# Seven block products for eight in the output matmul of a tuned kernel

What was changed: the second matmul of an expert block, `g @ w_out`, was made transposed for two batches at a time by Strassen's scheme. The block sums run on the vector engine, and the outputs are turned by 32x32 transposes on their way to memory.

## Chip, cores, metric

One core of one Trainium2 chip. The time is device microseconds (us) of a whole execution; a profiled execution also gives the span of the core, about 2 us less. Kernels that are compared ran on the same chip as runs of the kernel before. The engines are TensorE (PE), ScalarE (ACT), VectorE (DVE), GpSimd (POOL) and SyncE (SP, which only issues transfers here).

## The reference, cut

```python
# x: (8, 8, 512, 64) = batch, head, token, depth; state: (8, 8, 32, 64); all float32
scores = scale * x @ state^T;   a  = softmax(scores);   xread = a @ state
scores2 = scale * state @ x^T;  a2 = softmax(scores2);  sread = a2 @ x
y = concat([xread, sread], axis=tokens)    # (8, 544, 512) with the heads side by side
h = y @ w_in           # 512 x 2048
g = h * cos(h)
out = g @ w_out        # 2048 x 512, out is (4352, 512)
```

The weights arrive as float64 and are converted on the chip while batch 0 runs.

## The kernel before, the parts that matter

A batch (512 tokens) is worked in 16 steps, one per 128 columns of `w_in`. The attention of the next batch is cut into parts that stand in "slots" between the steps. In the traces each engine works through its instructions in the order in which the program names them: in batch 5 of the changed kernel the hidden tile named after the products starts behind them, at 607.45 us, although its buffer was read for the last time at 597.93.

```python
def hidden(t):                      # TensorE: h tile, 2 matmuls; only two h buffers
    for i in range(t.kn):
        nc.tensor.matmul(out=t.hp, lhsT=t.lhs(i), rhs=t.rhs(i), ...)
def gate(t):   nc.scalar.activation(t.q, t.hp, func=ACTF.Copy, bias=MAGIC)
def gate2(t):  nc.vector.scalar_tensor_tensor(out=t.q, ...)      # q = round(h) - h
def gate3(t):  nc.scalar.activation(..Abs); nc.scalar.activation(..Sin)
def gate4(t):  nc.vector.tensor_tensor(t.g, t.hp, t.q, op=ALU.mult)

def output(t):                      # TensorE: 4 matmuls per step, a few steps later
    for i in range(nt):
        nc.tensor.matmul(out=acc[i], lhsT=t.g[:, P * i:P * i + P],
                         rhs=w_out[:, t.f, :],
                         start=(t.f == 0), stop=(t.f == NF - 1))
    # ... after the last step: ACT evacuates acc[i], one DMA stores 128 rows of 2 KB

# parts of the attention of the next batch, in this order:
#   tokens 0..3, scores1, max2, spread1, shift, exps, sums, spread1, norm1   (EARLY)
#   turn 0,1, reads 0,1, keep, keep2                                         (LATE)
#   products 0..3                                                            (PRODS)
def products(self, nt, ...):        # 16 small matmuls into the one PSUM tile `at`
    self.per_head(stT, lambda rows, k: w_in[rows, k, cols], ...)
    nc.scalar.copy(sw_of[self.b, nt][...], at[...])
def exp2(self):                     # reads the same tile `at`
    nc.scalar.activation(self.z2[:, j], at[:, j], func=ACTF.Exp, ...)
def keep2(self):                    # transposes what keep (DVE) has just normalized
    nc.tensor.transpose(out=at[:, 1, 0:P], in_=self.sr..., identity=ident)
# ... the rest of the attention, the conversions and the loop are left out
```

In this kernel all four `products` of a batch come after its softmax; the pool of their results `sw` has six buffers.

## Time and profile before

| | before |
|---|---|
| time | 879.17 us median of 4 runs beside the changed kernel |
| span, PE busy, DVE busy, ACT busy | 877.2; 825.4; 330.8; 416.5 us |
| time of a steady batch (2 to 6) | 93.86 us, PE busy 93.86 us |

The page of the profile gives averages. More telling is a table of stretches: the span cut at the first gate instruction of each batch. The columns are start:end, length, then busy us (and count) of PE, weight loads, DVE, ACT and POOL, then the granted clock of TensorE as a fraction, the share of the DMA engines, and GB/s. Here are the starting stretch, batches 0 and 1, batch 4 and the rest after batch 7 (state tiles and end):

```profile
0.00:34.97 34.97, 12.53 (x60) 6.56 (x60) 17.29 (x26) 11.27 (x20) 3.13 (x10) 0.76 0.68 164
34.97:153.58 118.61, 96.72 (x362) 41.61 (x370) 86.22 (x113) 74.50 (x99) 0.00 (x0) 0.88 0.39 125
153.58:252.71 99.13, 97.40 (x379) 41.45 (x379) 32.06 (x47) 47.99 (x74) 0.00 (x0) 1.00 0.09 22
...
440.43:534.29 93.86, 93.86 (x331) 40.84 (x330) 31.94 (x47) 45.08 (x71) 0.00 (x0) 1.00 0.09 23
...
804.42:877.20 72.78, 67.06 (x216) 40.66 (x214) 13.52 (x32) 24.16 (x54) 0.00 (x0) 0.98 0.07 22
```

In batches 2 to 7 TensorE has no idle time at all. Apart from the start (22.4 us) and the end (5.7) it stands still only in batch 0, where the weights are converted, for 118.61 - 96.72 = 21.9 us, and for 1.7 us in batch 1.

### The profile page before, as it was taken

Reading aid. Unit: us, or ns where it says so; the run is one execution under the profiler, and the core shown is the slowest. Engines: PE = TensorE matmul, PEld = TensorE weight load, DVE = VectorE, ACT = ScalarE, POOL = GpSimd, SP = SyncE. Lnnn points to the kernel's source line nnn. Section 1 sums busy time; section 2 is a strip of 40 time slices with the busy share of each in tenths; the row PEclk is TensorE's granted clock in tenths of the full one; section 3 lists DMA queues with packets and bytes.
Section 4 is the critical chain, followed back from the end, with each engine's and each line's share of the span. In section 5 each row is a group of like instructions: output and inputs, shape, how many; then the busy total and the mean of one; then the engine's idle time right before and its main releaser. Section 6 shows DMA issues by size and latency. Waiting matters only on the chain.

```text
span 877.2 us, 7341 instructions
## 1 busy us (share of the span) xinstructions
PE 825.4 (94%) x2848; PEld 371.7 (42%) x2848; DVE 330.8 (38%) x485; ACT 416.5 (47%) x648; POOL 3.1 (0%) x10
## 2 busy tenths in 40 slices
PE   2549979999999999999999999999999999999997
PEld 1124334434444444444344434444444434445663
DVE  3666986244224422352224322442244222222121
ACT  2565674446345534463446444553446344433332
POOL 1000000000000000000000000000000000000000
PEclk8678989999999999999999999999999999999999
DMA  6743720030003000120003000300010001000100
GB/s 143 208 151 128 207 96 1 1 96 1 1 0 97 0 1 1 40 57 0 1 1 96 1 0 1 97 0 1 1 48 1 0 1 47 1 0 1 48 1 24
DMA packets 44418, 35.07 MB, mean 40 GB/s; under 512 B 35360, under 2 KB 35360, under 8 KB 44384
## 3 DMA queue, kind: packets, MB, share of 16 engines
q1 hardware_dynamic: 43168, 34.08, 13.6%
q10 hardware_dynamic: 1088, 0.26, 0.2%
q8 instruction: 22, 0.36, 0.2%
q0 software_dynamic: 128, 0.26, 0.1%
q14 instruction: 12, 0.10, 0.0%
HBM read 25.69 MB, written 8.91 MB: 39 GB/s over the span
## 4 chain that ended last, share of the span: by engine, by line
PE 88%; DVE 5%; ACT 5%; DMA 1%; issue 0%; SPq 0%; DVEq 0%; ACTq 0%
PE o L425 51%; PE h L395 28%; PE at L248 4%; PE at L325 2%; PE at L223 1%; PE at L310 1%; ACT q L410 1%; DMA x_b<-in_x_dram 1%; ACT q L409 1%; ACT e L166 1%; DVE q L404 1%; DVE w_in L183 0%; ACT q L401 0%; DVE m L261 0%; DVE w_out L183 0%; DVE spread L267 0%
## 5 line engine op out<-in xcount | busy, mean ns | idle before, releaser
L425 PE MATMUL o<-w_out,g 128*128 128x512 f32 x1088 | 494.3, 596 | 0.0
L425 PEld LDWEIGHTS o<-w_out,g 128*128 128x128 f32 x1088 | 203.4, 191 | 246.0 <-issue 242.7
L395 PE MATMUL h<-aT,sw 128*128 128x512 f32 x512 | 250.2, 612 | 0.2 <-ACT sw L357 0.2
L404 DVE SCALAR_TENSOR_TENSOR q<-q,h 128x512 f32<-128x512 f32 (+1 forms) x144 | 94.3, 655 | 333.0 <-ACT q L401 333.0
L401 ACT ACTIVATE q<-h 128x512 f32<-128x512 f32 (+1 forms) x144 | 82.5, 573 | 253.5 <-PE h L395 253.5
L415 DVE TENSOR_TENSOR g<-h,q 128x512 f32<-128x512 f32 (+1 forms) x144 | 95.2, 661 | 170.4 <-ACT q L410 170.3
L395 PEld LDWEIGHTS h<-aT,sw 128*128 128x128 f32 x512 | 95.7, 195 | 119.4 <-issue 110.4
L409 ACT ACTIVATE q<-q 128x512 f32<-128x512 f32 (+1 forms) x144 | 87.2, 606 | 107.6 <-DVE q L404 107.5
L410 ACT ACTIVATE q<-q,halfpi 128x512 f32<-128x512 f32 (+1 forms) x144 | 100.5, 698 | 4.5
L248 PE MATMUL at<-w_in,stT 64*32 64x512 f32 (+1 forms) x512 | 37.0, 620 | 8.4 <-ACT z L287 4.7
L357 ACT COPY sw<-at 128x1024 f32<-128x1024 f32 (+1 forms) x32 | 31.6, 987 | 24.9 <-PE at L248 24.9
L395 PE MATMUL h<-sT,w_in 128*128 128x256 f32 x128 | 30.2, 379 | 0.0
L431 ACT ACTIVATE ot<-o 128x512 f32<-128x512 f32 x34 | 19.3, 591 | 20.8 <-DMA out_dram<-ot 13.9
L395 PEld LDWEIGHTS h<-sT,w_in 128*128 128x128 f32 x128 | 24.3, 190 | 10.1 <-issue 5.3
L223 PE MATMUL at<-ident,x_b 128*128 128x128 f32 x112 | 17.9, 285 | 9.0 <-ACT xT L230 8.7
L223 PEld LDWEIGHTS at<-ident,x_b 128*128 128x128 f32 x112 | 14.3, 146 | 23.7 <-issue 11.6
L230 ACT COPY xT<-at 128x512 f32<-128x512 f32 x28 | 16.0, 572 | 10.5 <-PE at L223 10.5
L248 PEld LDWEIGHTS at<-w_in,stT 64*32 64x32 f32 x512 | 6.1, 107 | 34.8 <-issue 12.9
L267 DVE STREAM_TRANSPOSE spread<-m 128x1024 f32<-128x1024 f32 x16 | 19.8, 1235 | 0.0
L166 ACT ACTIVATE e<-raw 128x1024 f32<-128x1024 uint32 (+1 forms) x18 | 18.8, 1044 | 0.0
L325 PEld LDWEIGHTS at<-x_b,a2T 128*64 128x64 f32 x256 | 13.6, 136 | 12.1 <-issue 10.6
L325 PE MATMUL at<-x_b,a2T 128*64 128x128 f32 x256 | 17.5, 279 | 0.0
(53 smaller groups left out, 256.1 us busy)
## 6 DMA issues: line engine op xcount, KB each, us to landing
x_b<-in_x_dram SPq DMA_DIRECT2D x32, 256.0 KB, 4.7
raw<-in_moe_w_out_dram SPq DMA_DIRECT2D x8, 1024.0 KB, 4.9
out_dram<-ot SPq DMA_DIRECT2D x32, 256.0 KB, 2.1
raw<-in_moe_w_in_dram SPq DMA_DIRECT2D x6, 1024.0 KB, 5.3
raw<-in_moe_w_in_dram SPq DMA_DIRECT2D x4, 512.0 KB, 6.5
out_dram<-ot SPq DMA_DIRECT2D x8, 64.0 KB, 1.7
st<-in_state_dram ACTq DMA_DIRECT2D x4, 64.0 KB, 4.4
st<-in_state_dram POOLq DMA_DIRECT2D x4, 64.0 KB, 5.7
```

Source lines behind the costliest of these rows:

```text
L166: nc.scalar.activation(e, raw.bitcast(U32)[:, :, :, 0], func=ACTF.Copy, scale=2.0 ** -51, bias=2.0)
L223: nc.tensor.transpose(out=out[:, P * c:P * c + P], in_=self.x_b[:, c, 2 * k:2 * k + 2, :], identity=ident)
L248: nc.tensor.matmul(out=(to[j] if to else at[:, j])[Ns * k:Ns * k + Ns, 0:n], lhsT=w[D * j:D * j + D, self.b, Ns * k:Ns * k + Ns], rhs=r(sl ...
L325: nc.tensor.matmul(out=at[rows, 0, cols], lhsT=self.a2T[:, j, c, rows], rhs=x_c[:, j, k:k + 2], start=(c == 0), stop=(c == NC - 1), tile_p ...
L357: nc.scalar.copy(sw_of[self.b, nt][:, :, c0:c1], at[:, :, 0:c1 - c0])
L395: nc.tensor.matmul(out=t.hp, lhsT=t.lhs(i), rhs=t.rhs(i), start=(i == 0), stop=(i == t.kn - 1))
L401: nc.scalar.activation(t.q, t.hp, func=ACTF.Copy, bias=MAGIC)
L404: nc.vector.scalar_tensor_tensor(out=t.q, in0=t.q, scalar=MAGIC, in1=t.hp, op0=ALU.subtract, op1=ALU.subtract)
L409: nc.scalar.activation(t.q, t.q, func=ACTF.Abs)
L410: nc.scalar.activation(t.q, t.q, func=ACTF.Sin, bias=halfpi, scale=-TWO_PI)
L415: nc.vector.tensor_tensor(t.g[:, 0:t.n], t.hp, t.q, op=ALU.mult)
L425: nc.tensor.matmul(out=acc[i], lhsT=t.g[:, P * i:P * i + P], rhs=w_out[:, t.f, :], start=(t.f == 0), stop=(t.f == NF - 1))
```

## The change

The intent: TensorE is the bound, so do an eighth less of its output work. Two batches form a pair. The 2x2 blocks are batch by half of the hidden columns on one side and halves of `w_out` on the other. Seven products of blocks replace eight; the price is 128 subtractions of 128x512 on DVE, sums of weight blocks made once, more evacuations, and an output that comes out transposed.

A pair has four phases of eight steps: even batch first and second half (0, 1), odd batch first and second half (2, 3). Two products are put off: P7 (with the weight sum `s3`) and P4 (with the block `a22`) run beside phases 0 and 1 of the next pair, or beside the state tiles after the last one. Output follows its step by three steps.

```diff
-    swp = ctx.enter_context(tc.tile_pool(name="swp", bufs=6))
-    ops = ctx.enter_context(tc.tile_pool(name="ops", bufs=4, space=PSUM))
+    swp = ctx.enter_context(tc.tile_pool(name="swp", bufs=2))
+    ops = ctx.enter_context(tc.tile_pool(name="ops", bufs=1, space=PSUM))
+    acc = ops.tile([P, 2, 2, S], F32, name="o")      # banks MAIN and SIDE
 def output(t):
-    for i in range(nt):
-        nc.tensor.matmul(out=acc[i], lhsT=t.g[:, P * i:P * i + P],
-                         rhs=w_out[:, t.f, :], ...)
+    if t.phase == 0:
+        if product(MAIN, a11, t, i):
+            keep_product(pr.u, MAIN)
+        if pr.before:
+            p7(pr.before, i)
+    if t.phase == 1:
+        last = product(MAIN, a12, t, i)
+        if pr.before:
+            p4(pr.before, i)
+        # ... evacuate, store
+    if t.phase == 2:
+        if product(MAIN, s1, pr.b[0, i], i):
+            keep_product(pr.p5, MAIN)
+    if t.phase == 3:
+        last = product(MAIN, s2, pr.b[0, i], i)
+        product(SIDE, s4, t, i)
+        # ... evacuate, store
+def product(bank, w, g, i):         # 2 matmuls of 128x512 instead of 4 per step
+    for ch in range(2):
+        nc.tensor.matmul(out=acc[:, bank, ch], lhsT=w[:, i, P * ch:P * ch + P],
+                         rhs=g.g, start=(i == 0), stop=(i == NH - 1))
+def sums(t):                        # DVE: the block sums, in place in g
+    if t.phase == 2:
+        minus(pr.b[0, i].g, t.g, pr.b[0, i].g)
+    if t.phase == 3:
+        minus(pr.b[0, i].g, t.g, pr.b[0, i].g)
+        minus(pr.b[2, i].g, t.g, pr.b[2, i].g)     # and one more in sums2
+def store(b, half, ch, src):        # DVE 32x32 transposes, then rows of 32 floats
+    nc.vector.transpose(out=ot..., in_=src[:, ch]...)
+    nc.sync.dma_start(out=rows[:, :, c0:c0 + 32], in_=ot[32 * q:32 * q + 32]...)
+# slots of a batch b >= 1; two slots to a step:
+    at_ = {1: (b, "products", 1), 11: (b, "products", 2),
+           18: (b, "products", 3), 26: (b + 1, "products", 0)}
+    at_.update(zip((2, 3, 4, 5, 6, 7, 8, 9, 10, 12, 13, 14), E))
+    at_.update(zip((15, 16, 19, 20, 21, 22), L))
 # ... weight layout, conversions, state tiles and the tile generator are left out
```

With room for only two `sw` buffers, the products of a batch now stand among the softmax of the next one. `exps` is in slot 10 and `products 2` in slot 11.

## The prediction

> **What bounds the kernel now.** I read the page's busy times and slices first, then the costliest groups, then the timeline of TensorE, ScalarE (ACT) and VectorE (DVE) over some steady tiles and over the start.
>
> ```profile
> PE 825.4 (94%) x2848; PEld 371.7 (42%) x2848; DVE 330.8 (38%) x485; ACT 416.5 (47%) x648; POOL 3.1 (0%) x10
> PE   2549979999999999999999999999999999999997
> L425 PE MATMUL o<-w_out,g 128*128 128x512 f32 x1088 | 494.3, 596 | 0.0
> L395 PE MATMUL h<-aT,sw 128*128 128x512 f32 x512 | 250.2, 612 | 0.2 <-ACT sw L357 0.2
> ```
>
> TensorE is full from about 120 us to the end. Each matmul of the program leaves two records: the 544 output matmuls show as x1088. In the timeline the eight records of one tile's four output matmuls occupy 3.43 us, so **one output matmul costs 0.858 us**; the two hidden ones cost 1.72 us. A tile is 5.15 us of TensorE. A steady batch lasts 93.86 us (first gate instruction of batch 3 at 346.57, of batch 4 at 440.43): 16 x 5.15 = 82.4, plus 11.46 of attention (batch 7, which prepares nothing, lasts 82.4).
>
> Now the gate, which runs through ACT and DVE in turn:
>
> ```profile
> 401.92 0.60 ACT L401 ACTIVATE q<-h 128x512 f32<-128x512 f32 x1 [2.38 <-PE h L395]
> 402.55 0.69 DVE L404 SCALAR_TENSOR_TENSOR q<-q,h 128x512 f32<-128x512 f32 x1 [2.76 <-ACT q L401]
> 403.27 0.63 ACT L409 ACTIVATE q<-q 128x512 f32<-128x512 f32 x1 [0.75 <-DVE q L404]
> 403.93 0.72 ACT L410 ACTIVATE q<-q,halfpi 128x512 f32<-128x512 f32 x1
> 404.68 0.69 DVE L415 TENSOR_TENSOR g<-h,q 128x512 f32<-128x512 f32 x1 [1.45 <-ACT q L410]
> ```
>
> From the start of q to the end of g are 3.45 us. From one L404 to the next, when nothing else intervenes, are 0.72 + 0.66 + 0.75 + 0.61 = 2.75 us: **the gate loop**. Only two h buffers exist, and TensorE executes in order, so it can never be more than two tiles ahead of g. Today 2.75 against 5.15 leaves 2.4 us per tile, in which attention's ACT and DVE work hides. Where it does not hide, the start shows what happens:
>
> ```profile
> 48.23 1.11 PE L223 MATMUL at<-ident,x_b 128*128 128x128 f32 x4 [4.67 <-ACT xT L230]
> 118.30 1.96 PE L248 MATMUL at<-w_in,stT 64*32 64x512 f32 x16 [4.74 <-ACT z L287]
> ```
>
> The first says that two users of the tile `at` are serialized by the ACT copy of the first, though they use different banks. The second says that products placed behind the exponentials wait for these, because the exponentials read `at`.
>
> [...](691 for L415, 1218 for the 1024-wide L304 between SBUF tiles). So a block subtraction of 128x512 costs 0.69 us, spaced 0.61 (0.72 behind a result it needs). [...]exp follows sine's end after 1.3 us (284.16 to 285.48)[...]. I use the trace: load 1.28, exponentials 3.6 to 3.7 together, and another load ahead of the next sine. [...]after the 4.74 us above, the x16 group takes 1.96 us in place of 1.09. [...]the instruction order of the changed program keeps such waits.
>
> **The change, part by part.** I call one hidden tile a step, 16 to a batch.
>
> *Removed:* per pair of batches 128 output matmuls become 7 x 8 x 2 = 112, so 16 x 0.858 = 13.7 us, in four pairs **54.9 us**. If TensorE stayed full: 879 - 55 = 824.
>
> *Where it is removed:* two of the seven products of a pair move into the next pair's first batch (after batch 7: into the state tiles). So a TensorE step is 5.15 us in even batches, but in odd batches, steps 3 to 10, it has one product alone: 4 x 0.858 = 3.43 us. In the first pair it is 3.43 until step 11 of batch 1.
>
> *Added on DVE:* per pair 8 + 3 x 8 = 32 subtractions, 14 evacuations and totals, 8 transposes, 54 x about 0.65 = 35 us, or 140 us altogether, plus eight weight sums of 1.2 us and two more weight conversions. DVE goes from 331 to about 480 us, far from full. But in odd batches the subtractions lie in the gate loop: 2.75 + 0.71 = 3.46 us in steps 0 to 7 and about 4.75 in steps 8 to 15. So **in steps 3 to 10 loop and TensorE are even and all hiding room is gone**.
>
> *An odd batch that prepares a next one (3 and 5).* Time from the end of step 2's last product. DVE must do four evacuations, g, a subtraction and a store transpose, so gate2 of step 3 starts at 4.6. Then the loop carries max (1.2), row max (1.35), two to three transposes (0.65 each) and shift (1.2): sine of step 5 ends at 17.3. The exponentials end at 21.0. In the new order the products stand right behind them on TensorE, ahead of the next hidden tile; TensorE, finished at 12.0, idles **9 us**. Later in the same batch the transposes of step 8 wait for an ACT copy (2.0), the reads of step 9 for a copy behind a sine (2.0), the last transpose for the normalization on DVE (2.0). Sum 15, with a cold clock after the long gap about 17. The saving was 13.7.
>
> *An even batch (2, 4, 6):* at step 5 products wait for the exponentials, sine's end at 2.8 after TensorE's hidden tile plus 3.7, against 3.43 of products: 3.0 us. At step 10 four DVE evacuations precede g and the normalization, on which a transpose waits: 3.2 us. Sum 6.2. *Batch 7* prepares nothing: 1 us.
>
> *First pair.* A conversion step's loop is 2.75 + 2.6 (three DVE instructions ahead of gate2) = 5.35; pairs of `at` users cost 2.5 more. With 12 conversions, four plain steps, attention and a first step of 10.4, batch 0 takes 110 us against 118.6 (q at 34.97 to 153.58). Batch 1 has two conversions and seven weight sums in its loop besides: 52 to 54 us for steps 0 to 7, about 44 for the rest, 98 against 99.1. The first pair thus gains about 9 of its 41 us.
>
> *Sum.* Gate2 of batch 2 at 253.3 - 9 = 244. Batches 2 to 5: even 93.9 + 6.2 = 100, odd 80.1 + 15 = 95, twice 195, to 634. Batch 6: 100; batch 7: 68.6 + 3.7 + 1 = 73; to 807. From there the kernel before needs 72.2; add 32 matmuls of the two late products, 27.5, less 3.4 for a lag of three tiles in place of four: 903. Profile span to time is +2: **905**. Cold clocks would add some 5, slack that I missed takes away; I say 904.
>
> **Rivals.** *A: TensorE stays full.* For it: DVE at 38% and ACT at 47% have room on average, and the long phases have 5.15 us of TensorE a step. Against it: averages say nothing of an in-order loop with two h buffers. It gives 824 to 840. *B: only the loop in odd batches binds, copies and products mostly hide.* Losses would be about 6 us per odd batch and 20 in the first pair: about 860 to 880. For it: steady waits on `at` did not stop TensorE before. Against it: these had four output matmuls, 3.43 us, between them, now one pair, 1.72. *C: stores bind.* Outputs now leave in rows of 32 floats, 128 B, and DVE's transpose waits for one of two store buffers. If a group of four transfers takes over 6 us, several waits of a few us come into the loop at each of 16 groups: up to 925. Against it: input rows of 256 B came at about 200 GB/s, and transposes of one buffer are some 5 us apart. *D: the evacuations hold PSUM banks.* From the order a hidden tile and often another product lie between, so under 1 us each time.
>
> **Range and chances.** My sum of waits is 80 us against 55 saved, and its terms are chains, each good to perhaps a fifth; the first pair is uncertain by 8. Range 868 to 926. That a change built with so much care was tuned to pay speaks for A or B more than the profile does, hence faster 0.14, same 0.29, slower 0.57.
>
> **What would show it.** Right: TensorE busy near 770 us but at 84 to 87% of the span; output matmul records 960 in place of 1088; batches 3 and 5 each around 95 us and even ones around 100 between first gates; inside odd batches TensorE waiting for z about 9 us before `at` products, once a batch; in even ones about 3; the state tiles after batch 7 about 96 us. Wrong: no waits for z over 4 us outside batch 0 (A), odd batches near 85 (B), or DVE waiting for DMA in front of the transposes (C).

## The result

The changed kernel takes **954.26 us** (952.74 to 954.66, 4 runs) against 879.17: ratio 1.085 (95% interval 1.083 to 1.087), so 8.5% slower. Ratios here are the mean time of one kernel's fast runs over that of the other's of the same rounds, so not quite the ratio of the quoted medians. The direction of the prediction held; the time lies 28 us above its range.

The page of the changed kernel: busy times, TensorE's slices, and the two groups of output matmuls of batches (mean ns of one after the busy time).

```profile
PE 797.4 (84%) x2720; PEld 350.9 (37%) x2720; DVE 482.4 (51%) x725; ACT 410.4 (43%) x634; POOL 3.1 (0%) x10
...
PE   3367667857998989689999899589989899899997
...
L464 PE MATMUL o<-g_all,w_out 128*128 128x512 f32 x512 | 237.8, 604 | 6.1 <-ACT held L476 3.5
...
L464 PE MATMUL o<-g_all,s 128*128 128x512 f32 x384 | 176.9, 596 | 3.5 <-ACT held L476 2.7
```

The 512 + 384 records here and 64 of the state tiles are the 960 predicted, so the work did fall. But TensorE is busy only 28.0 us less, not 54.9, and its slices have holes all along the span. The span grew by 75.7 us: idle time went from 51.8 to 155.5 us (+103.7), and busy time took back 28.0.

How much of the missing 26.9 us of busy time is clock can be estimated from the traces: in each window of 0.5 us, busy time times the missing part of the granted clock is what a full clock would have saved. From the first gate on these add up to 31.5 us in the changed kernel and 11.0 in the kernel before, **20.5 us more**. (The start is left out: the changed kernel's trace gives a clock of 1.00 there, up to 38.47 us, although four transposes take 1.12 us that take 0.66 later.) The start itself has 1.6 us more busy time; 4.8 us stay without a name.

The stretches after, for batches 0, 1, 4, 5, 7 and the rest:

```profile
38.47:161.82 123.35, 82.50 (x311) 33.99 (x312) 81.42 (x108) 73.34 (x100) 0.00 (x0) 0.83 0.41 128
161.82:260.81 98.99, 77.71 (x286) 32.55 (x285) 69.13 (x99) 45.78 (x70) 0.00 (x0) 0.97 0.09 16
...
464.60:568.65 104.05, 95.89 (x330) 41.15 (x329) 40.78 (x63) 44.38 (x68) 0.00 (x0) 0.98 0.12 21
568.65:665.89 97.24, 83.22 (x298) 35.42 (x297) 56.78 (x88) 43.93 (x69) 0.00 (x0) 0.95 0.13 22
...
769.99:846.40 76.41, 72.86 (x213) 31.29 (x212) 46.62 (x72) 34.08 (x54) 0.00 (x0) 1.00 0.17 42
846.40:952.90 106.50, 93.59 (x272) 51.63 (x270) 31.83 (x59) 26.14 (x54) 0.00 (x0) 0.97 0.11 20
```

| stretch | before | predicted | after | PE idle before | PE idle after |
|---|---|---|---|---|---|
| start | 35.0 | 35 | 38.5 | 22.4 | 24.4 |
| batch 0 | 118.6 | 110 | 123.4 | 21.9 | 40.9 |
| batch 1 | 99.1 | 98 | 99.0 | 1.7 | 21.3 |
| batches 2, 4, 6 | 93.9 each | 100 each | 106.6, 104.1, 104.1 | 0 | 8.2 each |
| batches 3, 5 | 93.9 each | 95 each | 97.2 each | 0 | 14.0 each |
| batch 7 | 82.4 | 73 | 76.4 | 0 | 3.6 |
| rest | 72.8 | 96.3 | 106.5 | 5.7 | 12.9 |

What TensorE waited for, in the summary of waits (what <- the releaser: us in total, times, longest):

```profile
PE at L274 <- ACT xT L315: 41.7, 7, 8.7
PE at L371 <- DVE sr L365: 17.1, 7, 3.0
PE at L339 <- ACT xT L342: 12.0, 5, 4.8
...
PE h L417 <- ACT sw L386: 7.9, 3, 3.3
...
PE o L572 <- DVE w_out L221: 4.1, 2, 2.1
...
PE o L572 <- DVE held L470: 2.3, 1, 2.3
```

The first line is the products (L274) waiting for the exponentials (L315), once in each of batches 0 to 6; the second is `keep2` (L371) waiting for the normalization `keep` (L365). The other lines are smaller: an attention transpose and hidden tiles behind ACT, and the state tiles' outputs behind DVE.

The timeline shows one such wait from near. It gives start, duration, engine, line, output<-inputs, shapes, count, and in brackets the idle time before it and what ended it. First batch 4 (even), then batch 5 (odd):

```profile
501.95 1.96 PE L274 MATMUL at<-w_in,stT 64*32 64x512 f32 x16 [3.10 <-ACT xT L315]
...
541.32 0.33 PE L371 MATMUL at<-ident,sr 128*128 128x128 f32 x1 [3.04 <-DVE sr L365]
...
605.56 1.96 PE L274 MATMUL at<-w_in,stT 64*32 64x512 f32 x16 [8.72 <-ACT xT L315]
607.45 3.78 PE L417 MATMUL h<-aT,sw 128*128 128x512 f32 x4
```

In batch 5 TensorE stands for 8.72 us; then, its clock having fallen (granted 0.50 from 605.56 to 607.50 us), the 16 products take 1.96 us (1.09 at full clock) and the hidden tile 3.78 (1.88 at full clock). So one wait costs twice: idle time, and busy time that looks like work.

### The profile page after: what moved, and what is told of

It is laid out like the page before. It is cut to its first block, busy times and chain, and to the rows that moved or that the text cites. A ratio compares the mean times of both kernels' runs of the same rounds, so it can differ in the third digit from the quotient of the medians.

```text
span 952.9 us, 7331 instructions
## 1 busy us (share of the span) xinstructions
PE 797.4 (84%) x2720; PEld 350.9 (37%) x2720; DVE 482.4 (51%) x725; ACT 410.4 (43%) x634; POOL 3.1 (0%) x10
## 3 DMA queue, kind: packets, MB, share of 16 engines
q10 hardware_dynamic: 1088, 0.26, 0.2%
## 4 chain that ended last, share of the span: by engine, by line
PE 65%; DVE 19%; ACT 12%; issue 1%; DMA 1%; SPq 0%; DVEq 0%; ACTq 0%
PE o L464 33%; PE h L417 22%; PE at L274 4%; PE o L572 3%; DVE q L426 3%; ACT q L432 3%; DVE held L470 2%; ACT q L431 2%; DVE g_all L441 2%; DVE g_all L438 2%; PE at L354 1%; ACT q L423 1%; ACT xT L315 1%; DVE xT L293 1%; ACT L310 1%
## 5 line engine op out<-in xcount | busy, mean ns | idle before, releaser
L417 PE MATMUL h<-aT,sw 128*128 128x512 f32 x512 | 261.3, 635 | 9.6 <-ACT sw L386 7.9
L464 PE MATMUL o<-g_all,w_out 128*128 128x512 f32 x512 | 237.8, 604 | 6.1 <-ACT held L476 3.5
L426 DVE SCALAR_TENSOR_TENSOR q<-q,h 128x512 f32<-128x512 f32 (+1 forms) x144 | 93.9, 652 | 253.3 <-ACT q L423 253.0
L423 ACT ACTIVATE q<-h 128x512 f32<-128x512 f32 (+1 forms) x144 | 82.4, 572 | 274.6 <-PE h L417 274.6
L464 PE MATMUL o<-g_all,s 128*128 128x512 f32 x384 | 176.9, 596 | 3.5 <-ACT held L476 2.7
L438 DVE TENSOR_TENSOR g_all<-h,q 128x512 f32<-128x512 f32 (+1 forms) x144 | 94.8, 658 | 132.0 <-ACT q L432 131.9
L464 PEld LDWEIGHTS o<-g_all,w_out 128*128 128x128 f32 x512 | 97.0, 195 | 130.3 <-issue 117.3
L464 PEld LDWEIGHTS o<-g_all,s 128*128 128x128 f32 x384 | 71.3, 191 | 92.8 <-issue 85.0
L274 PE MATMUL at<-w_in,stT 64*32 64x512 f32 (+1 forms) x512 | 42.3, 705 | 54.1 <-ACT xT L315 41.7
L441 DVE TENSOR_TENSOR g_all<-g_all 128x512 f32<-128x512 f32 x128 | 83.2, 688 | 3.2
L470 DVE SCALAR_TENSOR_TENSOR held<-o,held 128x512 f32<-128x512 f32 x40 | 25.9, 687 | 41.8 <-PE o L464 41.5
L572 PE MATMUL o<-w_out,g_all 128*128 128x512 f32 x64 | 31.3, 621 | 6.4 <-DVE w_out L221 4.1
L274 PEld LDWEIGHTS at<-w_in,stT 64*32 64x32 f32 x512 | 6.4, 112 | 80.1 <-ACT xT L315 47.5
L488 DVE STREAM_TRANSPOSE ot<-held 128x512 f32<-128x512 f32 x32 | 22.3, 696 | 1.3 <-DMA out_dram<-ot 1.2
```

The costliest lines, as they stand in the source:

```text
L274: nc.tensor.matmul(out=(to[j] if to else at[:, j])[Ns * k:Ns * k + Ns, 0:n], lhsT=w[D * j:D * j + D, self.b, Ns * k:Ns * k + Ns], rhs=r(sl ...
L417: nc.tensor.matmul(out=t.hp, lhsT=t.lhs(i), rhs=t.rhs(i), start=(i == 0), stop=(i == t.kn - 1))
L426: nc.vector.scalar_tensor_tensor(out=t.q, in0=t.q, scalar=MAGIC, in1=t.hp, op0=ALU.subtract, op1=ALU.subtract)
L441: nc.vector.tensor_tensor(out, a, b, op=ALU.subtract)
L464: nc.tensor.matmul(out=acc[:, bank, ch], lhsT=w[:, i, P * ch:P * ch + P], rhs=g.g, start=(i == 0), stop=(i == NH - 1))
L470: nc.vector.scalar_tensor_tensor(out=out[:, ch], in0=acc[:, bank, ch], scalar=TWO_PI, in1=b[:, ch], op0=ALU.mult, op1=ALU.add)
```

## The experiments

My theory (W): the added time is waits of TensorE that the order of the program makes, because a step with two matmuls fewer no longer covers the chains that stand in it, and the cold clock after them. Rivals: the load of DVE (L), false dependencies between parts of one tile (F), and the stores in rows of 128 B (S). S needs no run: the page has the transposes into the two store buffers waiting for transfers only 1.2 us in the whole span (the last pair of numbers is idle time before the group, and what ended most of it).

```profile
L488 DVE STREAM_TRANSPOSE ot<-held 128x512 f32<-128x512 f32 x32 | 22.3, 696 | 1.3 <-DMA out_dram<-ot 1.2
```

All kernels gave correct results unless said otherwise. The kernel before measured 879.2 to 879.8 us beside each.

**Products two slots later.** Only the order of the program changes, from batch 1 on.

```diff
-        at_ = {1: (b, "products", 1), 11: (b, "products", 2),
+        at_ = {1: (b, "products", 1), 13: (b, "products", 2),
-        at_.update(zip((2, 3, 4, 5, 6, 7, 8, 9, 10, 12, 13, 14), E))
+        at_.update(zip((2, 3, 4, 5, 6, 7, 8, 9, 10, 11, 12, 14), E))
```

> One part moved: from batch 1 on, the third products of a batch stand one step later, no longer directly behind the exponentials (sums and spread take the freed places). Theory W (waits in the in-order chain, each followed by a cold clock): the 3.1 us wait plus about 1.9 us of cold matmuls in each of batches 2, 4, 6 goes, and some 6 us in each of batches 1, 3, 5, because only the gate loop with its table load remains there: 15 + 18 = 33 us, so about 921. Rival D (VectorE simply has too much to do in the odd batches; the wait would turn up elsewhere): odd batches keep their 97 us and the time stays above 940.

Measured 922.6 us (920.2 to 924.5), ratio 1.049. That is 31.7 us for moving one entry of a list, with the work of every engine unchanged; W had forecast about 921. Batches 1 to 6 got 6.0, 7.3, 5.5, 4.8, 5.4 and 4.8 us shorter. In batch 4 the wait is gone; in batch 5 it is 3.87 us where it was 8.72, still with a cold clock behind (1.96 us for 1.09):

```profile
581.40 1.96 PE L274 MATMUL at<-w_in,stT 64*32 64x512 f32 x16 [3.87 <-ACT xT L315]
```

**No block sums.** The result is wrong; 128 DVE subtractions are left out.

```diff
-            sums(t)
+            t.pair.b[t.phase, t.i] = t
-            sums2(t)
```

> Wrong result on purpose: the 128 subtractions of g blocks (83 us of VectorE) are left out, all else stays. Theory W: only the subtraction in the gate loop of steps 3 to 7 of odd batches (0.71 us each) and some of steps 8 to 10 can matter: 4 to 6 us per odd batch, 15 to 22 us in all, so 932 to 939. Rival D (VectorE's load is the bound): most of the 83 us goes, under 890.

Measured 933.4 us (932.5 to 935.7). Taking away 83.2 us of DVE work gives 20.9 us, within the 15 to 22 of W; batches 3 and 5, where the sums stand in the gate loop, got 5.4 and 5.8 us shorter. So the sums cost something, but their load is not the bound; moving a list entry gave more.

**State outputs split to exact ranges.** In the state tiles each output matmul read both halves of `w_out`, while DVE was converting parts of one half. Here each matmul reads one half.

```diff
-            nc.tensor.matmul(out=acc[:, MAIN, i], ..., rhs=w_out[:, :, t.f, :])
+            for m in range(2):
+                to = (acc[:, MAIN, m] if i == 0 else at[:, m])[:, 0:HD]
+                nc.tensor.matmul(out=to, ..., rhs=w_out[:, m, t.f, :])
```

> The state tiles' output matmuls read each half of w_out by itself (two matmuls of 256 columns for one of 512, into four half banks). If the two 2.06 us waits for the late weight conversions at state steps 8 and 9 are false dependencies, because a read over both halves spans the half that is being converted, they go, with the cold clock behind them: steps 8 and 9 lasted 10.9 and 9.2 us where the others took 6.87, so 6 us less, 948. If the waits are real (the conversion's data are needed there) the time stays at 953 to 955.

Measured 947.0 us (944.3 to 947.8), 7.2 less. The two waits of 2.06 us are gone, and the sixteen state tiles, first to last gate, take 86.95 us where they took 93.20. In the changed kernel they looked so:

```profile
900.86 3.41 PE L572 MATMUL o<-w_out,g_all 128*128 128x512 f32 x4 [2.06 <-DVE w_out L221]
904.06 3.91 PE L464 MATMUL o<-g_all,w_out 128*128 128x512 f32 x8
...
911.76 1.98 PE L572 MATMUL o<-w_out,g_all 128*128 128x512 f32 x4 [2.06 <-DVE w_out L221]
```

The same data were ready without the wait, so it was a false dependency (F): one read over both halves waited 2.06 us for the conversion, and two reads of one half each did not. The same fence shows the clock: one wait of 2.06 us is followed by 3.41 us (granted clock 0.57) for a group that takes 1.98 (1.00) after the other.

**Idle matmuls to keep the clock up.** Nine matmuls whose result nobody reads are put ahead of the products of batches 1, 3 and 5, into the wait.

```diff
+            if n == 11 and t.b in (1, 3, 5):
+                for _ in range(9):
+                    nc.tensor.matmul(out=acc[:, 1, 0], lhsT=a11[:, 0, 0:P], ...)
```

> Work added: nine idle output matmuls (7.7 us of TensorE, into two banks' worth of accumulator that nobody uses then) in front of the products that wait 7.6 to 8.7 us for the exponentials in batches 1, 3 and 5. If the cold clock after such a wait costs what the records say (products 1.96 for 1.09, next hidden tile 3.78 for 1.88), each of the three batches gets about 2.8 us shorter: 945 to 947. If only the wait itself counts, the time stays at 953 to 955 or rises.

Measured 950.9 us, but in two groups of runs (953.97, 954.17 and 947.88, 947.42), so the total alone says little. The trace, of the 953.97 run, says more. Batches 3 and 5 took 94.78 and 94.70 us in place of 97.19 and 97.24, **2.5 us less each although work was added**, because this follows in batch 5:

```profile
604.66 1.09 PE L274 MATMUL at<-w_in,stT 64*32 64x512 f32 x16 [1.18 <-ACT xT L315]
605.69 1.98 PE L417 MATMUL h<-aT,sw 128*128 128x512 f32 x4
```

Batch 1, the third one with idle matmuls, gained nothing (99.1 for 99.0): its first half got 1.5 us shorter and its second 1.6 longer. That run lost the rest of the gain elsewhere: batch 0 was 1.0 us longer and batch 6 2.9. What makes the two groups was not tested. One thing was seen here twice: one wait, followed by a cold group in one place and by a warm one in another (2.06 us above, and 3.10 us below). What makes that difference was not tested either.

**First products ahead of a conversion.** At the start the products of the second half of a weight group waited 4.21 us for a conversion of other columns.

```diff
                 convert3(3)
+                part(0, "products", 0, HC, WC)
                 convert1(conv)
-            at_ = {1: (0, "products", 0, HC, WC), 7: ...
+            at_ = {7: ...
```

> The block products of batch 0's second half weight group are put out before conversion 4 instead of behind it, so that the 4.2 us wait of PE for the conversion of another part of w_in, which these products do not read, can fall away. If that wait was a false dependency (the ranges of the two column groups interleave, so that they are taken to overlap): the first stretch of batch 0 gets 4 us shorter, with the cold clock after it perhaps 6, so 948 to 950 us against 954. If the products really need that conversion or the wait is replaced by one for the data itself: 953 to 955, and the wait stays at about 4 us in the trace under the conversion that writes these columns.

Measured 953.5 us (952.0 to 955.6): no gain, a miss. The wait was false, but it covered a true one. Here are the two waits in the changed kernel:

```profile
46.45 1.10 PE L274 MATMUL at<-w_in,stT 64*32 64x256 f32 x12 [4.21 <-DVE w_in L221]
...
56.60 1.12 PE L339 MATMUL at<-ident,xT 128*128 128x128 f32 x4 [4.79 <-ACT xT L342]
```

and here the next of them in the experiment:

```profile
55.71 1.11 PE L339 MATMUL at<-ident,xT 128*128 128x128 f32 x4 [8.03 <-ACT xT L342]
```

The transposes (L339) need an ACT copy that comes no sooner; 4.21 us of waiting became 3.24 more at the next place.

**Copies ahead of conversions.** In batch 0 the ACT passes of the next weight conversion stood ahead of the copies of `sw`, for which hidden tiles wait.

```diff
-        if nxt is not None:
-            convert0(nxt)
         go(2 * (step % NF))
 ...
             sums2(t)
+        if nxt is not None:
+            convert0(nxt)
```

> The first two passes of each weight conversion on the scalar engine are moved to the end of the step, behind the copies of the products. If batch 0's hidden tiles waited (1.8, 2.8, 3.3 us) only because those copies stood behind the conversion in the scalar engine's order: these waits fall to under 1 us, 946 to 949 us. If the conversion's own chain takes their place (its vector passes of the next step now wait for the scalar passes): the waits move to the gate and the time stays at 953 to 956.

Measured 949.6 us (948.3 to 950.1), 4.6 less, just outside the 946 to 949 hoped for. Waits of hidden tiles for the copies fell from 1.76, 2.84 and 3.29 us to 1.19, 0.79 and 0.93; a wait for the gate, 1.67 us before, became 2.81. Batch 0 became 115.0 us for 123.4, but batch 1 rose from 99.0 to 102.7; why it took back part of the gain was not tested.

**The single-product phase moved.** The previous pair's P4 goes from phase 1 to phase 2, so that the short steps stand in the second half of even batches and not where the softmax of an odd batch stands. It needs a fourth `held` buffer and, for room, one slot of `g_all` less and one buffer less of small tiles.

```diff
-            if pr.before:                 # phase 1
-                p4(pr.before, i)
+            if pr.before:                 # phase 2
+                p4(pr.before, i)
```

> The phase that has only one block product per step is moved from the first half of each odd batch (where the next batch's attention chain stands) to the second half of each even batch: the previous pair's P4 goes from phase 1 to phase 2. The work of every engine is the same. If the odd batches lost 14 us to waits because their steps are too short to cover the in-order chain (3.4 against 5.2 us of PE work): batches 3 and 5 fall to the waits of the even ones, 8 to 9 us, and batches 2, 4, 6 stay within 2 us of theirs less the moved work, so 4 to 7 us less per pair from batch 2 on, in all 940 to 947 us. If the waits depend on the chain alone and not on where the short steps stand, or come back in the second half (turns and reads): 952 to 957.

Measured 945.8 us; three runs at 945.6 to 947.5, one at 937.7. By the trace of a 946.0 run, batches 2 and 3 together fell from 203.8 to 200.8 us and batches 4 and 5 from 201.3 to 198.0. That is 3 us a pair, not the 4 to 7 of W, and batches 6 and 7 together did not gain (180.6 us for 180.5). Another 3.3 us of the gain lie in batch 0, where no product was moved: the time is in W's range partly by luck. The mechanism shows in the trace. In an odd batch, now with two products a step there, the wait for the exponentials falls from 8.72 us to 3.28:

```profile
588.75 1.96 PE L274 MATMUL at<-w_in,stT 64*32 64x512 f32 x16 [3.28 <-ACT xT L315]
```

TensorE's idle time in batches 3 and 5 falls from 14.0 to 9.9 us each; two new waits of 1.14 us for an ACT copy, one of 1.18 for a bank and a longer one for the normalization (3.16 for 1.86) take part of it back.

**The last transpose one slot later.** `keep2` follows the output products of its step and not the normalization directly.

```diff
-        at_.update(zip((15, 16, 19, 20, 21, 22), L))
+        at_.update(zip((15, 16, 19, 20, 21, 23), L))
```

> Only the last transpose of the attention part (it waited 3.0 us in even and 1.9 us in odd batches for the normalization on the vector engine, 17 us in all) is put one slot later, behind the output products of its step. If the wait is one of order, 1.3 us or nothing of it is left, and with the colder clock after it the time falls by 10 to 16 us, to 938 to 944. If the time that it covers is needed by something else in the step (the gate, the evacuations): under 5 us, 949 or more. With the mends measured one by one (32, 7, 1, 5, 8 us) this one would have to give about 17 for the sum to be the 70 us of the kernel with all of them.

Measured 934.2 us (933.8 to 937.0): 20.0 less, more than either theory said. The second halves of batches 1 to 6 shrank by 18.5 us in all; 15.8 of these are its waits there, which are gone. Another gain came from a place that the edit does not touch. In batch 4 the wait for the exponentials is again 3.10 us, but now the clock had not fallen:

```profile
491.43 1.09 PE L274 MATMUL at<-w_in,stT 64*32 64x512 f32 x16 [3.10 <-ACT xT L315]
```

and the first halves of batches 2, 4 and 6 took 52.8, 51.1 and 51.1 us for 53.9, 52.7 and 52.8. That these 4.4 us come from the clock is a guess that no run tests. Batch 0, also untouched, got 1.4 us shorter; the start, the first half of batch 1 and the state tiles gave 3.5 us back.

**All mends together.**

All edits above except the idle matmuls and the missing sums.

> All mends at once: products of the third weight group two slots later, state outputs split to the exact ranges, the first products early, conversions behind the copies, the single-product phase moved, and the last transpose of the attention part one slot later (its PE wait was 3.0 and 1.9 us, 17 us in all). If the lost time is these in-order waits and the cold clock behind them, the gains (measured 32 and 7, hoped for 4, 6, 8 and 15 to 20 us) add up to about 75 to 80 us: 870 to 885 us, about the time of the kernel before the change. If Strassen's scheme has another cost that none of them touches (vector engine load, stores in 128 byte rows): the sum falls short, 900 us or more, with PE's waits short in the trace but its busy time still 27 us over the 770 us of its work at full clock.

Measured **884.0 us** (882.8 to 884.1), ratio 1.005 (1.003 to 1.007): within 2% of the kernel before, in the range of W (870 to 885), and still slower. The single gains, each against the 954.26 of the first round, add up to 31.7 + 20.0 + 8.4 + 7.2 + 4.6 + 0.8 = 72.7 us; together they gave 70.2. Here are the page's busy times, then the stretches of batches 0, 1, 4, 5 and the rest:

```profile
PE 782.4 (89%) x2784; PEld 358.2 (41%) x2784; DVE 482.1 (55%) x725; ACT 410.6 (47%) x636; POOL 3.1 (0%) x10
```

```profile
39.02:153.76 114.74, 80.68 (x312) 32.90 (x313) 81.74 (x109) 73.57 (x99) 0.00 (x0) 0.87 0.45 138
153.76:243.69 89.93, 76.93 (x285) 32.45 (x284) 67.47 (x97) 45.44 (x71) 0.00 (x0) 0.98 0.10 18
...
425.50:514.58 89.08, 85.73 (x310) 36.78 (x309) 41.24 (x64) 44.04 (x68) 0.00 (x0) 1.00 0.14 24
514.58:607.27 92.69, 89.23 (x318) 38.29 (x317) 56.48 (x88) 43.95 (x68) 0.00 (x0) 1.00 0.14 23
...
779.88:881.10 101.22, 93.21 (x336) 64.56 (x334) 31.96 (x59) 26.41 (x56) 0.00 (x0) 0.98 0.13 21
```

DVE and ACT work is within 0.3 us of that of the changed kernel and the output matmuls are the same but for the split of the state tiles' (64 records more), yet PE is busy 15.0 us less (782.4 for 797.4). By the same estimate as above the clock takes 13.8 us of busy time from the first gate on, where it took 31.5 (or a little more than 13.8: the page of this trace shows a clock of 0.9 or more up to 44 us, although a hidden tile at 35.36 us took 3.62 us that takes 1.88 at 72.07). Steady pairs now gain (181.8 us for 187.7). What is left is read from the stretches and has no run of its own: in batch 0 TensorE is spared 16.0 us of busy time (80.7 for 96.7), but the stretch, full of weight conversions, shrinks by only 3.9. The two products put off there come back one pair after the other, at last in the state tiles, where TensorE has few holes: 28.4 us more (101.2 for 72.8), 26.2 of it busy. The start is 4.0 us longer too. Much of the saving falls where TensorE was idle anyway.

**More of the same.** A few entries moved on (the products of batch 1 to slot 15, the fourth products of batch 0 to 23, turns and `keep2` one later).

```diff
-        at_ = {1: (b, "products", 1), 13: (b, "products", 2),
+        at_ = {1: (b, "products", 1), 15 if b == 1 else 13: (b, "products", 2),
-        at_.update(zip((15, 16, 19, 20, 21, 23), L))
+        at_.update(zip((16, 17, 19, 20, 21, 24), L))
 # batch 0: products 3 in slot 23 for 22, the second spread1 in 22 for 23
```

> On top of all mends: in batch 1 the third products go two slots later still (their wait was 4.1 us in the trace of the mended kernel), in batch 0 the fourth ones one slot later (5.7 us, behind the exponentials), the turns and the last transpose of the attention part one slot later (1.3 us three times). If what is left of the waits is only order: 6 to 9 us less, 875 to 879 us, just under the kernel before. If these waits only move to the next instruction that needs the same results: 882 to 885.

Measured 893.0 us (891.4 to 894.2), **9 us worse**, a miss. In batch 1 the wait for exponentials went, but the copy of the products now came right before the hidden tile that reads it, which waited longer than the products had (4.11 us in the kernel with all mends):

```profile
203.65 3.78 PE L417 MATMUL h<-aT,sw 128*128 128x512 f32 x4 [7.66 <-ACT sw L386]
```

Batch 0 got 2.5 us longer, batch 1 5.9, batches 3 and 5 1.1 each. A slot can be too late as well as too early.

**Mended without sums**, on the kernel just named (wrong result):

> The mended kernel without the 128 block sums on the vector engine (the result is wrong on purpose). In the changed kernel their removal gave 21 us of time for 83 us of vector work. If the order of the work is what made them cost anything: in the mended kernel their removal gives under 6 us. If the vector engine's load itself holds the kernel up: again 15 to 21 us, about 860.

Measured 886.7 us (886.4 to 889.2), 6.4 less than that kernel: slightly over the bound I had given W, and far from the 15 to 21 of L. With a better order, the same 83 us of DVE work cost 6 us and not 21.

**A control on the kernel before**: its conversions, too, behind the copies.

```diff
                 convert3(conv)
-                convert0(conv + 1)
             gate3(t)
 ...
             gate4(t)
             go()
+            if conv:
+                convert0(conv + 1)
```

> A control on the kernel before the change: it too has the scalar passes of the next weight conversion ahead of the gate and of the copies in batch 0; here they go to the end of the step. If batch 0's waits came from the change's own order: no gain, 878 to 881 us. If the kernel before had the same fault: batch 0 gets 3 to 6 us shorter, 873 to 877 us, and the mended kernel has to be held against that.

Measured 878.7 us (875.9 to 879.3), ratio 0.998 (0.997 to 1.000): no gain worth the name. The mended kernel stands fairly against 879.

## Why the prediction was wrong in size

*What held.* The removed work (960 records), the PE share (84%), and DVE and stores not binding. The chains named are those that stop TensorE: waits of products for the exponentials were predicted as 9 us in odd and 3.0 in even batches, and measured 8.72 and 3.10; the last transpose in even batches 3.2, and measured 3.04; the three later waits of an odd batch 2.0 each, and measured 1.84, 1.60 and 1.86. The stations of the chain fit too, so this was not luck: counted from the end of step 2's products in batch 5, the sine of step 5 ended at 16.9 us (17.3 predicted), the exponentials at 20.6 (21.0), TensorE's work at 12.0 (12.0). Rival A (TensorE full) and rival B (odd batches alone lose, about 6 us) are refuted by these waits, rival C by the 1.2 us, and the two moved list entries (31.7 and 20.0 us) show that the waits set the time. Rival D (under 1 us each time) held in part: the waits for banks were 0.86 and 1.18 us in even batches, but 0.86 and 2.69 in batch 7 and 2.31 in the state tiles.

*What failed* are terms of the sum. By stage the misses are 3.5 us (start), 13.4 (batch 0), 1.0 (batch 1), 14.8 (the even batches together), 4.4 (batches 3 and 5), 3.4 (batch 7) and 10.2 (the rest), 50.7 us in all; the clock is inside several of them.

- **The cold clock.** The prediction says "Cold clocks would add some 5, slack that I missed takes away". It had TensorE busy near 770 us and it was 797.4; by the estimate above 20.5 us of the difference are clock. In batches 3 and 5 it was 2.5 us each by the idle-matmul run, in batch 2 4.3 and in batches 4 and 6 1.7 each by the same estimate. The prediction counted only the long gap of odd batches as cold, and left it out of its sum there; waits of 2.06 to 3.10 us were at times enough.
- **Batch 0** (110 predicted, 123.4 found, the largest miss of one stage, 13 us). The step "a conversion step's loop is 2.75 + 2.6" counted the gate loop, and left out that TensorE's hidden tiles wait for ACT copies queued behind the conversions' ACT passes (1.76, 2.84 and 3.29 us); nor does it name the exponentials' wait, 7.45 us where the kernel before had 4.74. Moving the ACT passes took 8.4 us off batch 0; some of it came back in batch 1. By the estimate 4 us of the miss are clock (15.0 us of busy time for 11.0); the rest was not taken apart by a run.
- **The state tiles** (96.3 predicted, 106.5 found). "From there the kernel before needs 72.2; add 32 matmuls" left out the two weight conversions that the change puts there, with their false dependencies (6.3 us by the split), and a wait of 2.31 us for the evacuation of the last batch's bank.
- **The even batches.** Sum 6.2 predicted; the waits are 8.2 (the bank waits of 0.86 and 1.18 in addition), with the clock on top: 104 to 107 for 100.
- **Batch 7**, 3.4 us longer than predicted: its waits for banks are 0.86 and 2.69 us by the trace, where the prediction had 1 us for all. **The start**, 3.5 us longer, was not taken apart.

In the steady batches the sum was made of waits that each proved right to a few tenths, and it set "slack that I missed" against the cold clock. No such slack showed: where TensorE was the bound, the waits found in the order were paid, and some were paid again in clock.

*What stays open.* Two things changed at once: short steps, and a new order with the products next to the exponentials. The traces separate them in part. Even batches have as many matmuls a step as before, and still wait 8.2 us where they waited 0; 2.0 of it are the waits for banks, and the two larger waits, 3.10 and 3.04 us, went when one entry each was moved. That part is the order. In odd batches the wait for the exponentials was 8.72 us with short steps and 3.28 with full ones. The new order with the old eight products was not run.

## What to carry to other kernels

Before cutting work from the bounding engine, look at what hides behind that work: here four output matmuls per step covered most of a softmax chain, and with two of them gone the wait for it was 8.72 us in place of 3.28. Then look at the order of issue: products right behind the exponentials waited even in full steps (3.10 us), and two list entries were worth 32 and 20 us of a loss of 75, against 21 for leaving out the 128 block sums (83 of the 152 us of added vector work). And ask where the saved work stood: in batch 0, full of weight conversions, 16.0 us less of busy time shortened the stretch by 3.9 (the kernel with all mends), and in its last stretch, where TensorE has few holes, 26.2 us more of it came with 28.4 us of time.

## What the traces show of the hardware

- TensorE's clock after a wait: groups at a lower clock followed waits of 3.10 us (1.96 us for 1.09, granted clock 0.50) and of 2.06 us (3.41 for 1.98, granted clock 0.57), and warm ones followed waits of the same lengths elsewhere. In all the cold clock took 31.5 us of PE busy time in a span of 952.9, by the estimate above.
- An fp32 matmul left two records in the profile: the 544 output matmuls of 128x128 by 128x512 leave 1088, and one takes 0.858 us at full clock.
- ACT_TABLE_LOAD took 1283 ns, and the exponential began 1.3 us after the end of the sine before it (284.16 to 285.48 in the kernel before).
- Stores in rows of 128 B landed after 2.0 us (median, 64 KB each) and delayed the kernel's transposes by 1.2 us in all.
- A read across two halves of a tile was held up by a conversion of part of one of them; it cost the state tiles 6.3 us.
